# Linear attention and a gated MLP on one core: a lane layout of five and four tokens, the value products moved to VectorE, the first loads on two queues, and an earlier output weight load

## The chip, the cores and the metric

The kernel runs on one core of a Trainium2 chip. The metric is the device time of one execution, in microseconds (us). Six names recur: PE is TensorE (PEld its weight load), DVE is VectorE, ACT is ScalarE, POOL is GpSimd, SP is SyncE, which here only issues DMAs. A name with a q behind it (SPq, ACTq, POOLq) is that engine's instruction queue, where DMAs are issued. A lane is one of the 128 partitions of the on-chip memory.

## The reference

Attention with 8 batches, 8 heads, 576 tokens and a head size of 64, with cosine and sine weights over the token's position and no softmax; its result goes through an RMS norm and a gated MLP (512 to 1536 and back).

```python
def phi(x, c, s):                       # c, s = cos, sin of pi/2 * position / 576
    r = np.maximum(x, 0.0)
    return np.concatenate([r * c, r * s], axis=-1)
q_p, k_p = phi(q, cos_w, sin_w), phi(k, cos_w, sin_w)
kv = np.einsum('bhsf,bhsd->bhfd', k_p, v)
z = np.sum(k_p, axis=2)
num = np.einsum('bhsf,bhfd->bhsd', q_p, kv)
den = np.einsum('bhsf,bhf->bhs', q_p, z)[..., None] + 1e-06
x = (num / den).transpose(0, 2, 1, 3).reshape(8 * 576, 512)
xn = x / np.sqrt(np.mean(x * x, axis=-1, keepdims=True) + 1e-06) * rms_g
g = xn @ w_gate
return (g * (1.0 / (1.0 + np.exp(-g))) * (xn @ w_val)) @ w_out
```

## The kernel before

**Tokens and lanes.** A batch has 576 tokens. The first 512 lie four to a lane over 128 lanes (`J = 4`, token 4p + j in lane p) and arrive in one DMA for each of v, k and q (lines 72 to 78 and 97 to 108; q of the first two batches in two parts). The remaining 64 tokens of a batch come in DMAs of their own: v and k into tiles of 64 lanes (`vrem`, `krem`, line 80), q of two batches into one tile of 128 lanes (`qrem`, line 110). All these loads are issued by SP, in the order of the program, except `vrem` and `krem` of batch 0, which ACT issues (lines 119 and 120).

**A batch's attention.** `k_feat` (line 233) takes the relu of k, on ACT, for batches 0 and 1 in part on DVE. `v_trig` (line 243) multiplies v by the cosine (c = 0) and by the sine (c = 1) of the token's position: on DVE, but for batches above 0 the sine half is on POOL (line 245). There are ten such products a batch, two for each of the five token columns. `kv_mm` (line 251) is 40 matmuls a batch, `kv_evict` copies the result out. `q_relu` and a transpose (by PE in batches 0 and 1, by DMA after that, `q_turn`, line 282) prepare q; `num_mm` (line 316) makes a tile of 128 tokens; `sin_part` on ACT and `cos_part`, `divide` on DVE finish it; `sumsq` needs ACT and then POOL for the power -0.5 (line 383, tile `rs`); `norm` (line 386) is DVE. The normed tile `xn` is transposed into `xnT`, by PE (`x_turn_pe`, line 401, with a copy by ACT or DVE) or by a DMA that SP issues (`x_turn`, line 394).

**The MLP.** Nine blocks of 512 tokens: block b holds the four tiles of batch b, block 8 the remaining tokens of all batches, two batches to a tile. A block has 12 steps. A step (line 606) makes one piece of the gate and one of the value product (`gps`, `vps`, three PSUM buffers), a silu on ACT, a product on DVE (`hT`, line 631), and from block 2 on four output matmuls of the block before (`out_mm`, line 453). Blocks 0 to 3 work on halves of 256 tokens (`HALVES`, line 598): the first six steps of blocks 1 to 3 need tiles 0 and 1 of the block, the last six tiles 2 and 3.

**Order.** It is written out by hand. The attention of batch 0 comes first, with idle matmuls (`warm_up`) between. Block 0 follows. Then comes `lead` (line 641): the attention of batch 1 up to three tiles, mixed with the 48 output matmuls of block 0. Steps are numbered g = 12 x block + step, so block 1 is steps 12 to 23 and block 2 begins with step 24. `at(g, list, ...)` hangs work on a step; within a step the lists run in the order sp, act0, dve0, transposes by DMA that are due (`x_turn_late`), the step's matmuls and silu, act1, dve1, the `hT` product, the output matmuls, pe. What is issued on one engine runs in this order.

**Loads beside it.** POOL issues the weight loads: gate and value thirds 0 and 1 once the last value product of batch 0 is done (line 710), thirds 2 at line 745, the three thirds of w_out in step 1 (`more_loads`, line 525). Behind these SP waits for the second third of w_out (`sp_after`, line 528) and then issues v, k, their rests and q of batch 1, and v, k and their rests of batch 2. q of batch 2 is issued in step 12, v and k of batch 3 in steps 15 and 16, q in step 20, v and k of batch 4 in steps 21 and 22. v and k have two buffers, q has one.

Of the kernel before, what the change touches and what calls it, by code (L numbers as in the profile page):

```python
# [10 lines left out]
FP32 = mybir.dt.float32  # L11
# [6 lines left out]
def kernel(  # L18
# [51 lines left out]
    kraw, vraw, qraw, kremt, vremt, qremt = {}, {}, {}, {}, {}, {}  # L70

    def load_main(src, b, name, pool, eng=nc.sync):
        t = pool.tile([P, H, J * D], FP32, name=name, tag=name)
        K(eng.dma_start(
            out=t[:, :, :],
            in_=src[b, :, 0:SM, :].rearrange("h (p j) d -> p h (j d)", j=J),
        ))
        return t

    def load_rem(src, b, name, eng=nc.sync):  # L80
        t = raw2.tile([R, H, D], FP32, name=name, tag=name)
        K(eng.dma_start(
            out=t[:, :, :], in_=src[b, :, SM:S, :].rearrange("h s d -> s h d")
        ))
        return t

    def load_v(b):
        vraw[b] = load_main(v, b, "vraw", raw2)

    def load_k(b):  # L90
        kraw[b] = load_main(k, b, "kraw", raw2)

    def load_kv_rem(b):
        vremt[b] = load_rem(v, b, "vrem")
        kremt[b] = load_rem(k, b, "krem")

    def load_q(b, parts=1):

        t = raw.tile([P, H, J * D], FP32, name="qraw", tag="qraw")
        jn = J // parts  # L100
        for o in range(0, J, jn):
            K(nc.sync.dma_start(
                out=t[:, :, o * D : (o + jn) * D],
                in_=q[b, :, 0:SM, :].rearrange("h (p j) d -> p h j d", j=J)[
                    :, :, o : o + jn, :
                ].rearrange("p h j d -> p h (j d)"),
            ))
        qraw[b] = t

    def load_q_rem(m):  # L110
        t = raw.tile([P, H, D], FP32, name="qrem", tag="qrem")
        for o in range(2):
            K(nc.sync.dma_start(
                out=t[o * R : (o + 1) * R, :, :],
                in_=q[2 * m + o, :, SM:S, :].rearrange("h s d -> s h d"),
            ))
        qremt[m] = t

    vremt[0] = load_rem(v, 0, "vrem", nc.scalar)
    kremt[0] = load_rem(k, 0, "krem", nc.scalar)  # L120
    load_v(0)
    load_k(0)
    load_q(0, 2)


    iota_i = consts.tile([P, 1], mybir.dt.int32, name="iota_i")
    nc.gpsimd.iota(iota_i[:, :], pattern=[[0, 1]], base=0, channel_multiplier=1)
    iota_f = consts.tile([P, 1], FP32, name="iota_f")
    nc.vector.tensor_copy(out=iota_f[:, :], in_=iota_i[:, :])
    NC5 = J + 1  # L130
    th = consts.tile([P, 2, NC5], FP32, name="th")
    trig = consts.tile([P, 2, NC5], FP32, name="trig")
    ang = math.pi / 2.0 / float(S)
    for j in range(J):
        nc.vector.tensor_scalar(
            out=th[:, 1, j : j + 1], in0=iota_f[:, :], scalar1=float(J) * ang,
            scalar2=float(j) * ang, op0=ALU.mult, op1=ALU.add,
        )
    for o in range(2):
        nc.vector.tensor_scalar(  # L140
            out=th[o * R : (o + 1) * R, 1, J : J + 1], in0=iota_f[o * R : (o + 1) * R, :],
            scalar1=ang, scalar2=float(SM - o * R) * ang, op0=ALU.mult, op1=ALU.add,
        )
# [6 lines left out]
    def cosc(j, lo=0, hi=P):  # L150
        return trig[lo:hi, 0, j : j + 1]

    def sinc(j, lo=0, hi=P):
        return trig[lo:hi, 1, j : j + 1]
# [20 lines left out]
    def clear_pads(u):  # L175
        nc.gpsimd.memset(rk[u][J][R:P, :, :], 0.0)
        nc.gpsimd.memset(vx[u][J][R:P, :, :, :], 0.0)
        for j in range(NC5):
            n = P if j < J else R
            for c in range(2):  # L180
                nc.gpsimd.tensor_copy(
                    out=vx[u][j][0:n, :, c, D:E],
                    in_=trig[0:n, c, j : j + 1].unsqueeze(2).to_broadcast([n, H, 2]),
                )
# [43 lines left out]
    def kv_src(b, j):  # L228
        if j < J:
            return (kraw[b][:, :, j * D : (j + 1) * D], vraw[b][:, :, j * D : (j + 1) * D], P)  # L230
        return kremt[b][:, :, :], vremt[b][:, :, :], R

    def k_feat(b, j, dve=False):
        rkk, _, n = kv_src(b, j)
        dst = rk[b % 2][j][0:n, :, :]
        if dve:
            K(nc.vector.tensor_scalar(
                out=dst, in0=rkk, scalar1=0.0, scalar2=None, op0=ALU.max
            ))
        else:  # L240
            K(nc.scalar.activation(out=dst, in_=rkk, func=AF.Relu))  # L241

    def v_trig(b, j, c):
        _, rv, n = kv_src(b, j)
        eng = nc.gpsimd if b > 0 and c == 1 else nc.vector
        K(eng.tensor_scalar(  # L246
            out=vx[b % 2][j][0:n, :, c, 0:D], in0=rv,
            scalar1=(cosc, sinc)[c](j, 0, n), scalar2=None, op0=ALU.mult,
        ))
# [20 lines left out]

    def q_relu(b, t, dve=False):
        rq = rqp.tile([P, H, D], BF16, name="rq", tag="rq")
        src = qraw[b][:, :, t * D : (t + 1) * D] if t < J else qremt[b // 2][:, :, :]
        if dve:
            K(nc.vector.tensor_scalar(
                out=rq[:, :, :], in0=src, scalar1=0.0, scalar2=None, op0=ALU.max
            ))
        else:
            K(nc.scalar.activation(out=rq[:, :, :], in_=src, func=AF.Relu))
        rqs[b, t] = rq  # L280
# [47 lines left out]
    def sin_part(key, lo=0, hi=P):  # L328
        tmp = post2.tile([P, H, E], FP32, name="tmp", tag="tmp")
        K(nc.scalar.activation(  # L330
            out=tmp[lo:hi, :, :], in_=att[lo:hi, :, E:W], func=AF.Copy,
            scale=sinc(key[1], lo, hi),
        ))
        tmps[key] = tmp

    def cos_part(key, lo=0, hi=P):
        if key not in xa:
            xa[key] = post.tile([P, H, E], FP32, name="xa", tag="xa")
        K(nc.vector.scalar_tensor_tensor(  # L339
            out=xa[key][lo:hi, :, :], in0=att[lo:hi, :, 0:E],  # L340
            scalar=cosc(key[1], lo, hi), in1=tmps.pop(key)[lo:hi, :, :],
            op0=ALU.mult, op1=ALU.add,
        ))
# [99 lines left out]

    def out_store(blk, jt, osb):
        if blk < B:
            dst = out[blk * S : blk * S + SM, :].rearrange("(p j) m -> p j m", j=J)[:, jt, :]
            K(nc.sync.dma_start(out=dst, in_=osb[:, :]))
        else:
            for o in range(2):
                r0 = (2 * jt + o) * S + SM  # L450
                K(nc.sync.dma_start(out=out[r0 : r0 + R, :], in_=osb[o * R : (o + 1) * R, :]))
# [73 lines left out]
    def more_loads():  # L525
        for c in range(NG):
            load_wo(c)
        sp_after(wo[0:1, n4, 0:1])
        load_v(1)
        load_k(1)  # L530
        load_kv_rem(1)
        load_q(1, 2)
        load_v(2)
        load_k(2)
        load_kv_rem(2)

    at(1, "pe", more_loads)

# [15 lines left out]
    at(12, "sp", load_q, 2)  # L554
    for j, g in enumerate((13, 14, 15, 15, 16)):
        prep_at(g, 2, j)
    for t in range(J):
        at(15 + t, "act1", q_feat, 2, t)
    kv_at(17, 2)
    for t, g in enumerate((18, 19, 22, 24)):  # L560
        tile_at(g, (2, t), [(2, 0, P)], 2, t, t < 2)
    at(15, "sp", load_v, 3)
    at(16, "sp", load_k, 3)
    at(17, "sp", load_kv_rem, 3)
    at(20, "sp", load_q, 3)
    for j, g in enumerate((23, 24, 25, 26, 27)):
        prep_at(g, 3, j)
    for t in range(J):
        at(26 + t, "act1", q_feat, 3, t)
    kv_at(28, 3)  # L570
    for t, g in enumerate((29, 30, 32, 34)):
        tile_at(g, (3, t), [(3, 0, P)], 3, t)


    for b in range(4, B):
        g1, g2, g3 = NNT * (b - 1), NNT * (b - 2), NNT * (b - 3)
        for o, f in ((2, load_v), (4, load_k), (6, load_kv_rem)):
            at(20 + o // 2 if b == 4 else g3 + o + (4 if b == 5 else 0), "sp", f, b)
# [3 lines left out]
        for t in range(J):  # L582
            at(g2 + 9 + t, "act1", q_feat, b, t)
        kv_at(g2 + (11 if b == 4 else 10), b)
# [4 lines left out]
    for m, (gl, gf, gn) in enumerate(((33, 39, 44), (45, 51, 56), (56, 62, 68), (72, 82, 85))):  # L589
        at(gl, "sp", load_q_rem, m)  # L590
        at(gf, "act1", q_feat, 2 * m + 1, J)
        tile_at(gn, (2 * m + 1, J), [(2 * m, 0, R), (2 * m + 1, R, P)], B, m)
# [48 lines left out]
    def lead():  # L641
# [26 lines left out]
        q_relu(1, 3)  # L668
        outs(24, 30)
# [25 lines left out]
        divide((1, 2))  # L695

# [9 lines left out]
    warm_up(68)  # L706
# [58 lines left out]
    for c in range(2):  # L765
# [14 lines left out]
        for o, eng in enumerate((nc.sync, nc.scalar)):  # L780
            r0 = (2 * (J - 1) + o) * S + SM
            K(eng.dma_start(out=out[r0 : r0 + R, cs], in_=osb[o * R : (o + 1) * R, cs]))
# [28 lines left out]
```

## Time and profile before

| what | value |
|---|---|
| median of 3 runs | 348.25 us (347.69 to 348.96) |
| the profiled execution's own time | 349.69 us |
| its span, first to last instruction | 347.9 us |
| PE busy | 331.3 us |
| DVE, ACT, POOL busy | 201.9, 180.6, 92.2 us |
| DMA | 50.22 MB, mean 144 GB/s |
| granted TensorE clock | 0.995 |

Busy time is the time in which an engine had an instruction in work. Shares over the whole span say little here, since the kernel has an attention start, blocks in which attention and MLP share the engines, and late blocks that are almost only matmuls; so the views below are read by stretches of time, each counted from the start of the span. The granted clock is 1.00 in nearly all stretches, which means that nothing held TensorE back.

### The profile page before, as it was taken

What the parts mean: (1) busy time and instruction counts of PE and PEld (TensorE: products, weight loads), DVE (VectorE), ACT (ScalarE), POOL (GpSimd) and SP (SyncE); (2) the same over time, 40 slices, a digit from 0 to 9 for tenths busy, and PEclk for the clock granted to TensorE, in tenths of its full rate; (3) what the DMA queues carried; (4) which work ended last, traced back from release to release, by engine and by line L of the source; (5) the groups of instructions that cost most, each with busy time, mean ns of one, the idle gap of its engine ahead of it and who ended that gap; (6) DMA issues with size and microseconds to landing.
All of it is one profiled execution on the core that took longest, in us unless ns stands there. A gap on an engine that the chain in (4) does not pass through costs nothing.

```text
span 347.9 us, 6475 instructions
## 1 busy us (share of the span) xinstructions
PE 331.3 (95%) x2498; PEld 195.6 (56%) x2498; DVE 201.9 (58%) x362; ACT 180.6 (52%) x345; POOL 92.2 (27%) x116
## 2 busy tenths in 40 slices
PE   8779998979899999999999999999999999999995
PEld 6558854758677767777544444444444444444443
DVE  2885467765784887776668666864673352232210
ACT  1475337756566586655765576566544343323321
POOL 8433091560455264140514051400100000000000
PEclk9999999989999999999999999999999999999999
DMA  7999999778913998984399446224123011110024
GB/s 210 272 199 193 216 272 292 225 214 170 332 29 92 271 246 168 288 196 106 91 317 184 107 79 179 60 70 109 51 61 62 32 38 39 50 40 32 30 59 92
DMA packets 79424, 50.22 MB, mean 144 GB/s; under 512 B 43298, under 2 KB 74786, under 8 KB 79394
## 3 DMA queue, kind: packets, MB, share of 16 engines
q1 hardware_dynamic: 73426, 44.71, 51.7%
q0 software_dynamic: 4752, 4.72, 8.4%
q10 hardware_dynamic: 1216, 0.39, 0.6%
q8 instruction: 19, 0.31, 0.4%
q14 instruction: 11, 0.09, 0.1%
HBM read 38.01 MB, written 9.44 MB: 136 GB/s over the span
## 4 chain that ended last, share of the span: by engine, by line
PE 66%; POOL 8%; DMA 7%; issue 7%; DVE 6%; ACT 3%; SPq 1%; ACTq 0%; POOLq 0%; DVEq 0%
PE acc L461 20%; PE gps L423 16%; PE vps L423 15%; POOL vx L246 6%; PE gps L436 5%; PE vps L436 5%; DMA qraw<-in_q_dram 3%; PE att L320 3%; DMA wo<-in_moe_w_out_dram 3%; PE att L256 2%; POOL rs L383 2%; DMA vraw<-in_v_dram 2%; DVE xa L339 1%; ACT sq L378 1%; DVE xn L388 1%
## 5 line engine op out<-in xcount | busy, mean ns | idle before, releaser
L631 DVE TENSOR_TENSOR hT<-vps,sil 128x512 bf16<-128x512 f32 x108 | 74.4, 689 | 91.8 <-PE vps L423 62.0
L461 PE MATMUL acc<-wo,hT 128*128 128x512 bf16 x420 | 105.6, 379 | 0.0
L625 ACT ACTIVATE sil<-gps 128x512 bf16<-128x512 f32 x108 | 64.2, 595 | 79.0 <-PE gps L423 54.8
L383 POOL TENSOR_TENSOR rs<-ss,mhalf 128x1 f32<-128x1 f32 x36 | 20.3, 565 | 174.2 <-ACT sq L378 174.2
L461 PEld LDWEIGHTS <-hT 128*128 128x128 bf16 x420 | 40.7, 98 | 43.2
L436 PE MATMUL vps<-xnT,wv 128*128 128x256 bf16 x384 | 50.6, 276 | 1.1 <-DVE hT L631 1.1
L436 PE MATMUL gps<-xnT,wg 128*128 128x256 bf16 x384 | 50.7, 276 | 0.8 <-ACT xnT L414 0.7
L423 PE MATMUL gps<-xnT,wg 128*128 128x512 bf16 x192 | 49.5, 380 | 0.0
L423 PE MATMUL vps<-xnT,wv 128*128 128x512 bf16 x192 | 49.3, 379 | 0.0
L246 POOL TENSOR_SCALAR vx<-vraw,trig 128x512 bf16<-128x512 f32 x28 | 45.4, 1631 | 13.9 <-DMA vraw<-in_v_dram 13.9
L436 PEld LDWEIGHTS <-wg 128*128 128x128 bf16 x384 | 36.1, 99 | 9.5 <-issue 0.8
L436 PEld LDWEIGHTS <-wv 128*128 128x128 bf16 x384 | 37.9, 99 | 6.1 <-issue 1.5
L388 DVE SCALAR_TENSOR_TENSOR xn<-x,rs,gb 128x512 bf16<-128x512 f32 x36 | 32.7, 908 | 11.9 <-POOL rs L383 11.8
L423 PEld LDWEIGHTS <-wv 128*128 128x128 bf16 x240 | 23.5, 98 | 28.3
L339 DVE SCALAR_TENSOR_TENSOR xa<-att,trig,tmp 128x528 f32<-128x528 f32 (+1 forms) x40 | 30.5, 763 | 14.9 <-ACT tmp L330 13.9
L330 ACT ACTIVATE tmp<-att,trig 128x528 f32<-128x528 f32 (+1 forms) x40 | 28.0, 700 | 19.9 <-PE att L320 19.0
L423 PEld LDWEIGHTS <-wg 128*128 128x128 bf16 x240 | 21.8, 98 | 25.8
L467 ACT COPY osb<-acc 128x512 f32<-128x512 f32 x35 | 20.4, 583 | 25.8 <-PE acc L461 25.7
L378 ACT ACTIVATE sq<-x 128x513 f32<-128x513 f32 x36 | 22.6, 629 | 8.1 <-DVE x L365 7.8
L365 DVE TENSOR_TENSOR x<-xa,rec 128x512 f32<-128x512 f32 x36 | 24.9, 692 | 1.2
L246 DVE TENSOR_SCALAR vx<-vraw,trig 128x512 bf16<-128x512 f32 x36 | 20.5, 593 | 0.0
L241 ACT ACTIVATE rk<-kraw 128x512 bf16<-128x512 f32 x28 | 17.2, 624 | 3.4 <-DMA kraw<-in_k_dram 3.4
(54 smaller groups left out, 211.3 us busy)
## 6 DMA issues: line engine op xcount, KB each, us to landing
vraw<-in_v_dram SPq DMA_DIRECT2D x8, 1024.0 KB, 8.3
kraw<-in_k_dram SPq DMA_DIRECT2D x8, 1024.0 KB, 10.1
out_dram<-osb SPq DMA_DIRECT2D x32, 256.0 KB, 2.4
qraw<-in_q_dram SPq DMA_DIRECT2D x6, 1024.0 KB, 6.2
qraw<-in_q_dram SPq DMA_DIRECT2D x4, 512.0 KB, 10.6
wg<-in_moe_w_gate_dram POOLq DMA_DIRECT2D x3, 512.0 KB, 7.2
wv<-in_moe_w_val_dram POOLq DMA_DIRECT2D x3, 512.0 KB, 9.0
wo<-in_moe_w_out_dram POOLq DMA_DIRECT2D x3, 512.0 KB, 9.1
```

Source lines behind the costliest of these rows:

```text
L246: K(eng.tensor_scalar(out=vx[b % 2][j][0:n, :, c, 0:D], in0=rv, scalar1=(cosc, sinc)[c](j, 0, n), scalar2=None, op0=ALU.mult,))
L330: K(nc.scalar.activation(out=tmp[lo:hi, :, :], in_=att[lo:hi, :, E:W], func=AF.Copy, scale=sinc(key[1], lo, hi),))
L339: K(nc.vector.scalar_tensor_tensor(out=xa[key][lo:hi, :, :], in0=att[lo:hi, :, 0:E], scalar=cosc(key[1], lo, hi), in1=tmps.pop(key)[lo:hi, ...
L365: K(nc.vector.tensor_tensor(out=x[:, 0:DM].rearrange("p (s e d) -> p e s d", e=2, d=D), in0=a[:, :, 0:D].rearrange("p (e s) d -> p e s d", ...
L378: K(nc.scalar.activation(out=sq[:, :], in_=xs[key][:, :], func=AF.Square, scale=1.0 / math.sqrt(DM), accum_out=ss[:, :],))
L383: K(nc.gpsimd.tensor_tensor(out=rs[:, :], in0=ss[:, :], in1=mhalf[:, :], op=ALU.pow))
L388: K(nc.vector.scalar_tensor_tensor(out=xn[:, :], in0=xs.pop(key)[:, 0:DM], scalar=rss.pop(key)[:, :], in1=gb[:, :], op0=ALU.mult, op1=ALU. ...
L423: K(nc.tensor.matmul(ps[:, :], lhsT=w[:, dt, nn * P : (nn + 1) * P], rhs=xnT[blk][:, dt, :], start=(dt == 0), stop=(dt == NDT - 1),))
L436: K(nc.tensor.matmul(ps[:, i * HB : (i + 1) * HB], lhsT=w[:, dt, (n0 + i) * P : (n0 + i + 1) * P], rhs=xnT[blk][:, dt, hf * HB : (hf + 1) ...
L461: K(nc.tensor.matmul(acc[blk][:, :], lhsT=hT[blk][:, nn, jt * P : (jt + 1) * P], rhs=wo[:, nn, :], start=(nn == 0), stop=(nn == NNT - 1),))
L625: K(nc.scalar.activation(out=sil[:, :], in_=gp[:, :], func=AF.Silu))
L631: K(nc.vector.tensor_tensor(out=dst, in0=a, in1=c, op=ALU.mult))
```

## The change

The lanes hold tokens differently: 64 lanes hold five tokens each and 64 lanes four, so that the whole batch lies in one tile of five columns (the fifth is filled in 64 lanes only). Even batches have the five in lanes 0 to 63, odd ones in lanes 64 to 127. The loads of the remaining tokens go away. Each load is now two DMAs, one for 64 lanes, since the two halves have different strides; both are issued by SP, one behind the other, but for v and k of batch 0, where SP issues one half and ACT the other. Each store of an output tile of blocks 0 to 7 is two DMAs of 64 lanes as well. All value products are on DVE. The relu of the fifth column of q is done on DVE into tiles of its own. w_out's first third is issued at the end of step 0, and SP waits for that third, not for the second, before it issues the loads of batch 1. q of batch 2 is issued in `lead`; the eight value products and two relus of k of batch 2 stand at the end of `lead`, the rest of its preparation in steps 12 and 13. The matmuls of its `kv` move from step 17 to 14, its tiles from steps 18, 19, 22, 24 to 16, 18, 20, 22; the first two of them are transposed by DMA, as the others, and not by PE. q of batch 3 is issued in step 19, its tiles begin a step earlier. There are 60 idle matmuls at the start in place of 68.

```diff
-    def load_main(src, b, name, pool, eng=nc.sync):
...
+    FIVE = R * (J + 1)
+    FOUR = R * J
+    def halves(b):
+        if b % 2 == 0:
+            return ((0, 0, J + 1), (R, FIVE, J))
+        return ((0, 0, J), (R, FOUR, J + 1))
+    def load(src, b, name, pool, cuts=(0, J + 1), engs=(nc.sync, nc.sync)):
+        t = pool.tile([P, H, (J + 1) * D], FP32, name=name, tag=name)
+        for lo, hi in zip(cuts[:-1], cuts[1:]):
+            for (l0, t0, jn), eng in zip(halves(b), engs):
+                a, z = min(lo, jn), min(hi, jn)
+                K(eng.dma_start(
+                    out=t[l0 : l0 + R, :, a * D : z * D],
+                    in_=src[b, :, t0 : t0 + R * jn, :].rearrange(
+                        "h (p j) d -> p h (j d)", j=jn
+                    )[:, :, a * D : z * D],
+                ))
         return t
...
-    vremt[0] = load_rem(v, 0, "vrem", nc.scalar)
-    kremt[0] = load_rem(k, 0, "krem", nc.scalar)
-    load_v(0)
-    load_k(0)
-    load_q(0, 2)
+    two = (nc.sync, nc.scalar)
+    load_v(0, engs=two)
+    load_k(0, engs=two)
+    load_q(0, cuts=(0, 2, J + 1))
...
     def v_trig(b, j, c):
-        _, rv, n = kv_src(b, j)
-        eng = nc.gpsimd if b > 0 and c == 1 else nc.vector
-        K(eng.tensor_scalar(
+        _, rv, lanes = kv_src(b, j)
+        K(nc.vector.tensor_scalar(
...
     def out_store(blk, jt, osb):
...
+        for l0, dst in rows:
+            K(nc.sync.dma_start(out=dst, in_=osb[l0 : l0 + R, :]))
...
     def more_loads():
-        for c in range(NG):
+        for c in range(1, NG):
             load_wo(c)
-        sp_after(wo[0:1, n4, 0:1])
+        sp_after(wo[0:1, 0, 0:1])
         load_v(1)
         load_k(1)
-        load_kv_rem(1)
-        load_q(1, 2)
+        load_q(1)
         load_v(2)
         load_k(2)
-        load_kv_rem(2)
-
+    at(0, "pe", load_wo, 0)
     at(1, "pe", more_loads)
+    at(1, "dve1", q_relu, 0, J, True)
...
-    at(12, "sp", load_q, 2)
-    for j, g in enumerate((13, 14, 15, 15, 16)):
-        prep_at(g, 2, j)
+    for j in (2, 3):
+        at(12, "dve1", k_feat, 2, j, True)
+    at(12, "act1", k_feat, 2, J)
+    for c in range(2):
+        at(13, "dve0", v_trig, 2, J, c)
+    kv_at(14, 2)
     for t in range(J):
-        at(15 + t, "act1", q_feat, 2, t)
-    kv_at(17, 2)
-    for t, g in enumerate((18, 19, 22, 24)):
-        tile_at(g, (2, t), [(2, 0, P)], 2, t, t < 2)
+        at(14 + t, "act1", q_feat, 2, t)
+    at(17, "dve1", q_relu, 2, J, True)
+    for t, g in enumerate((16, 18, 20, 22)):
+        tile_at(g, (2, t), [(2, 0, P)], 2, t)
     at(15, "sp", load_v, 3)
     at(16, "sp", load_k, 3)
-    at(17, "sp", load_kv_rem, 3)
-    at(20, "sp", load_q, 3)
-    for j, g in enumerate((23, 24, 25, 26, 27)):
+    at(19, "sp", load_q, 3)
+    for j, g in enumerate((22, 23, 24, 25, 26)):
...
-        at(26 + t, "act1", q_feat, 3, t)
-    kv_at(28, 3)
-    for t, g in enumerate((29, 30, 32, 34)):
+        at(24 + t, "act1", q_feat, 3, t)
+    at(27, "dve1", q_relu, 3, J, True)
+    kv_at(27, 3)
+    for t, g in enumerate((28, 30, 32, 34)):
...
     def lead():
...
         q_relu(1, 3)
+        q_relu(1, J, dve=True)
+        load_q(2)
         outs(24, 30)
...
         divide((1, 2))
+        k_feat(2, 0)
+        k_feat(2, 1)
+        for j in range(J):
+            for c in range(2):
+                v_trig(2, j, c)
...
-    warm_up(68)
+    warm_up(60)
```

## The prediction

> **What bounds the kernel now.** I read the page's head first, then the busy time by stages, then chain, waits and SP's queue in the early stages.
>
> ```profile
> PE 331.3 (95%) x2498; PEld 195.6 (56%) x2498; DVE 201.9 (58%) x362; ACT 180.6 (52%) x345; POOL 92.2 (27%) x116
> ...
> 0.00:23.00 23.00, 18.21 (x189) 13.69 (x190) 14.46 (x40) 8.79 (x16) 13.30 (x44) 1.00 1.04 232
> 23.00:45.70 22.70, 21.84 (x204) 19.29 (x203) 11.49 (x19) 10.65 (x20) 5.50 (x7) 1.00 1.10 217
> 45.70:63.40 17.70, 15.47 (x139) 7.82 (x137) 12.88 (x25) 10.11 (x20) 8.39 (x7) 1.00 1.04 269
> 63.40:94.80 31.40, 27.36 (x281) 21.94 (x282) 21.15 (x37) 20.28 (x40) 13.67 (x11) 0.95 0.85 235
> 94.80:131.80 37.00, 36.32 (x362) 26.37 (x359) 28.33 (x50) 24.15 (x49) 17.35 (x14) 1.00 0.75 160
> 131.80:332.70 200.90, 200.90 (x1273) 100.47 (x1270) 112.52 (x192) 103.89 (x197) 34.00 (x35) 1.00 0.43 103
> ```
>
> The stages are the start, block 0, `lead`, block 1, block 2 and the rest; columns: length, busy time of PE, PEld, DVE, ACT, POOL, granted clock, DMA share, GB/s. From 131.8 on PE never idles and the matmuls stay the same, so nothing can be won or lost there. All is decided before. PE lacks 0.9 us in block 0, 2.2 in `lead`, 4.0 in block 1 (whose clock of 0.95 costs 31.4 x 0.05 = 1.6 more) and 0.7 in block 2, and the first gate matmul comes only after 23 us. What it waits for:
>
> ```profile
> 3.65 11.42 DMA qraw<-in_q_dram
> 28.86 9.07 DMA wo<-in_moe_w_out_dram
> 38.76 5.42 DMA vraw<-in_v_dram
> 44.28 8.71 POOL vx L246 x5
> ...
> PE att L256 <- POOL vx L246: 1.6, 2, 1.1
> DVE rq L275 <- DMA qraw<-in_q_dram: 1.6, 1, 1.6
> ```
>
> The first four are the chain of work that ended last: the start hangs on the second part of q (landed at 15.07), `lead` on w_out, v and five POOL products. The waits are those of `lead`: the change removes the first, the second stays. DMA is the other limit: its share is above 1.0 up to 63.4, so how fast the loads run matters as much as the order.
>
> **The price of a half.** Every load becomes two DMAs of 64 lanes, one behind the other. The nearest rows are output stores, where the last block already writes 64 lanes at a time (windows: a load of 128 lanes, v of batch 1; a store of 128 lanes; two pairs of 64-lane stores; last, two 64-lane loads in 256-byte packets):
>
> ```profile
> 41.00:46.00 5.00, 5.00 (x47) 4.39 (x45) 1.83 (x4) 1.79 (x3) 1.72 (x2) 1.00 1.06 357
> 335.00:335.80 0.80, 0.80 (x6) 0.33 (x4) 0.00 (x0) 0.00 (x0) 0.00 (x0) 1.00 0.87 328
> 338.00:339.40 1.40, 1.40 (x8) 0.60 (x7) 0.00 (x0) 0.58 (x1) 0.00 (x0) 1.00 0.85 187
> 340.50:341.90 1.40, 1.40 (x11) 0.97 (x10) 0.00 (x0) 0.50 (x1) 0.00 (x0) 1.00 0.86 187
> 188.10:189.10 1.00, 1.00 (x7) 0.43 (x5) 1.00 (x3) 1.00 (x3) 1.00 (x2) 1.00 1.31 252
> ```
>
> The same 0.26 MB take 0.8 us as one store and 1.4 us as two halves. A load of v, k or q is now 576 x 512 x 4 bytes = 1.18 MB: 3.3 us at 357 GB/s, 4.7 at 252, 6.3 at 187. I take 5.6 us (210 GB/s, the mean of six 0.2 us windows inside the first pair: 225, 215, 184, 185, 236, 215), since that pair has the new loads' form; 3.3 and 6.3 are kept as ends. [...]
>
> **The start.** v and k of batch 0 come over two queues. Nearest is the stretch from 5 to 10 us, where ACT's queue loads 64 lanes beside SP's 128: 200 to 303 GB/s, mean 270. From the first packets at 2.8 us, 2.36 MB take 8.7 us at that rate: 11.5, against 11.75 (1.25 + 10.5) before. So v and k cost nothing, and 8 fewer idle matmuls nothing either; ends: 357 GB/s gains 2.1 us, 187 loses 3.9. Eleven small position instructions in place of eight end before 4 us, under the wait for v (DVE idle until 7.65). Then q on SP alone: 0.52 MB 2.5 us, 0.66 MB 3.1 us, so the second part lands at 11.3 + 5.6 + 0.4 = 17.3, which is 2.2 us late. DVE's relu of it stands ahead of two `rqT` copies and the first `cos_part`; what it lacks, all lack. The first weight loads run from 14.4 on, beside it. Between 14.4 and 15.2 the DMA view has
>
> ```profile
> q0 software_dynamic: 71, 0.07, 63.8%
> q1 hardware_dynamic: 76, 0.12, 44.6%
> ```
>
> packets of weights (q0) and SP's queue (q1) one for one; if that held, the part would land up to 6 us later still. I take **+2.2** and keep -1.7 (all at 357) and +8.
>
> **w_out in step 0** gains nothing by itself: POOL's `rs` at 27.35 (0.78 us) stands before it in either step, so it is issued at 28.1 as now. But SP waits for third 0, landed 6.9 us after issue, at 35.0, not for third 1 at 37.95. First packets of v then come at 37.6, 3 us earlier.
>
> **`lead`.** With 5.6 us a load the queue's data end: v 43.2, k 48.8, q 54.4, v of batch 2 60.0, k 65.6. The products of batch 1 on DVE take 8 x 0.41 (3.24 us for eight in the start) from 46.66: all ten are done by 51.7 with two relus between. POOL's chain ended at 53.0, so `kv` could be done 1.4 us sooner. It is of no use: q lands at 54.8, against 52.4, and `num_mm` follows it. `lead` ends 2.4 us later, at 65.8. The q relu of the fifth column (0.45 us) fits where DVE waits 1.6 us for `tmp`. If q came early the 1.4 us would be won.
>
> **Block 1.** ACT first waits for k of batch 2 (66.0), then two relus: silu of step 12 at 67.2. DVE, after `divide` at 66.8, has eight products (3.3), two relus (0.8), `hT` (0.6), `norm` (0.7): 72.2. Queued behind is the PE transpose of tile (1,2), which also needs the PSUM buffer that this `hT` frees: PE goes on at 72.6, some 2.6 us after it could. Afterwards DVE has fewer products than now, POOL's 3.3 us pairs are gone, and so is the 1.18 us `xn` beside them (0.74 alone). With matmuls of 0.87 us, step 24 would be due at 93.0.
>
> But two tiles of batch 2 are now transposed by DMA, in SP's queue. What it costs to stand behind a load there:
>
> ```profile
> 74.36 0.57 SPq L74 DMA_DIRECT2D kraw<-in_k_dram  x1
> 75.42 1.19 SPq L284 DMA_TRANSPOSE rqT<-rq  x1
> ```
>
> The first `rqT`, ahead of any load, landed after 2.5 us, this one after 5.5, with the k load (5.8 us). In the new order SP issues v3 (v of batch 3, step 15, 75.6), `rqT`, k3, two `rqT`, q3 (step 19), `xnT` of tile (2,0), v4 (step 21), `xnT` of tile (2,1). First packets 1.8 us after issue: 77.4, four loads 22.4, five transposes at 0.76 us (512 packets each, as in lone ones) 3.8: the last lands at **103.6**. Step 24 needs tiles (2,0) and (2,1). It began at 94.8: **+8.8 us**. Now the cover is that both go through PE, for 0.8 us.
>
> **The rest.** Block 2 loses its 0.7 us of PE idle (POOL pairs, `xn`): **-0.7**, or 0. Later blocks have 18 us of loads and 5.6 of stores in 31 us, and a tile is due 7.8 us after its last turn: hidden. The 32 added store DMAs (0.36 us of SP each) are covered by that slack too, and 22 issues of rests go. Eight relus of the fifth q column move to DVE (0.45 us each) and four leave ACT, in steps that last 2.6 us and in which both idle. The tail's stores stay as they are.
>
> Sum: 2.2 + 8.8 - 0.7 = +10.3 us on the profiled execution's 349.69 us (span 347.9 and 1.8 around it). That execution is 1.4 above the median of the runs; on the median, 348.25 + 10.3 = **358.5 us**.
>
> **Rivals.** (a) Halves run as fast as whole loads. Then the start gains 1.0 (within -1.7), `lead` 1.4, block 1 3.6 (PE's own 24.7 us + 2.6 + 0.5 against 31.4), block 2 0.7, and `xnT` is about 1 us late: -5.7, **342.5**. It decides where a load takes under some 4.1 us (287 GB/s; a straight line between the two sums). For it: 252 GB/s in the only load row above. Against it: 187 in the rows of the same form. (b) 4.7 us a load, as that row has: q costs nothing, the last transpose lands at 72.5 + 1.8 + 18.8 + 3.8 = 96.9, +2.1, the start +1, block 2 -0.7: **350.6**. (c) Two queues help v and k no more than one: at 187 GB/s k lands 3.9 us later and v 1.9, and with v's products the weight loads start 1.9 later, which q then meets less: +3 net, **361.5**. [...] (d) Loads are fast, but DVE becomes the bound of block 1: its 21.15 us lose 4.8 (products there, slow `xn`) and gain 10.2 (ten products 4.7, relus 1.3, a tile 2.3, batch 3's four 1.9), 26.6 against PE's 24.7, and weights meet q at the start: about **347.5**.
>
> **Chances.** Forecast 0.40, (a) 0.27, (b) 0.11, (c) 0.13, (d) 0.09. A measurement of this kernel can tell about 0.3% from no change. Faster: (a) and a third of (d), 0.30; within 0.3%: 0.06; slower 0.64. Range 341.5 to 364.0; the forecast's own 352 to 364.
>
> **What would show it.** GB/s near 200 while v of batch 1 loads, 5 us and more from one landing to the next; q's second part at 17 us; ACT waiting for `kraw` at the end of `lead`; and PE idle for 8 us before step 24 with `xnT` as releaser. Loads at 350 GB/s, or `xnT` landed before PE comes to step 24, would make the prediction wrong.

## The result and the profile after

The changed kernel takes **384.0 us** (median of 4 runs, 382.1 to 385.7) where the kernel before takes 348.61: a ratio of **1.102**, 95% interval 1.095 to 1.108. It is slower, and by 35 us where 10 were forecast. The profiled execution took 382.1 us, its span 380.3 against 347.9. The busy line of its page:

```profile
PE 334.4 (88%) x2449; PEld 198.3 (52%) x2482; DVE 209.6 (55%) x410; ACT 177.3 (47%) x337; POOL 34.2 (9%) x82
```

Its busy time by stages, cut at the same work as those of before (start, block 0, `lead`, blocks 1 and 2, rest; the same columns):

```profile
0.00:28.30 28.30, 19.76 (x182) 14.82 (x183) 16.27 (x44) 9.31 (x18) 12.85 (x45) 0.82 1.07 208
28.30:50.07 21.77, 21.58 (x201) 19.16 (x201) 10.90 (x18) 10.02 (x19) 3.56 (x5) 1.00 1.15 191
50.07:74.89 24.82, 16.70 (x135) 8.32 (x136) 13.69 (x31) 9.95 (x20) 1.10 (x2) 0.86 1.13 219
74.89:117.97 43.08, 27.33 (x280) 21.61 (x281) 28.25 (x59) 20.66 (x41) 2.92 (x5) 0.88 0.94 164
117.97:162.61 44.64, 37.12 (x346) 27.09 (x353) 24.99 (x50) 23.72 (x45) 2.19 (x4) 0.92 0.85 147
162.61:365.00 202.39, 200.78 (x1246) 101.28 (x1270) 114.38 (x207) 100.94 (x191) 11.60 (x21) 0.99 0.54 99
```

PE's work is nearly the same (334.4 us busy against 331.3), so most of the loss is waiting. The first cut above lies on the first gate matmul (28.30); the one of before lies 0.94 us ahead of it (23.00, the matmul at 23.94). Counted from that matmul in both, the start is 4.4 us longer, block 0 equal, `lead` 7.1 longer, block 1 11.7, block 2 7.6, and the rest with the last microseconds behind the table 1.6: together 32.4, the difference of the spans. Two columns belong together: the DMA share is as high as before or higher, yet the bytes of the start, block 0 and `lead` move at 191 to 219 GB/s and not at 217 to 269. The engines are as busy and move less. And the granted clock, 1.00 in nearly every stage of before, is 0.82 to 0.92 in four stages. What ended the waits stands in the chain, here the longest piece of four of its stretches (start and length in us),

```profile
8.61 10.15 DMA qraw<-in_q_dram
44.96 17.35 DMA qraw<-in_q_dram
104.99 12.85 DMA xnT<-xn
152.26 10.31 DMA xnT<-xn
```

and in the waits (total, times, longest):

```profile
PE gps L441 <- DMA xnT<-xn: 16.2, 2, 9.1
ACT rk L243 <- DMA kraw<-in_k_dram: 21.7, 3, 9.7
```

The waits of POOL's products that stood in `lead` are gone. In their place stand loads (q of batch 0 landing at 18.8 us, q of batch 1 at 62.3) and two transposes by DMA that PE waits for, 9.1 us before step 24 and 7.1 us before step 36.

### The profile page after: what moved, and what is told of

Its sections match the earlier page's. It is cut to its first block, busy times and chain, and to the rows that moved or that the text cites. A ratio compares the mean times of both kernels' runs of the same rounds, so it can differ in the third digit from the quotient of the medians.

```text
span 380.3 us, 6453 instructions
## 1 busy us (share of the span) xinstructions
PE 334.4 (88%) x2449; PEld 198.3 (52%) x2482; DVE 209.6 (55%) x410; ACT 177.3 (47%) x337; POOL 34.2 (9%) x82
## 4 chain that ended last, share of the span: by engine, by line
PE 70%; DMA 16%; DVE 6%; ACT 2%; SPq 2%; issue 2%; POOL 0%; ACTq 0%; DVEq 0%
PE acc L473 21%; PE gps L428 14%; PE vps L428 13%; PE gps L441 9%; PE vps L441 8%; DMA qraw<-in_q_dram 7%; DMA xnT<-xn 6%; PE att L325 3%; DMA rqT<-rq 2%; SPq L89 2%; PE att L257 1%; DVE vx L247 1%; DVE hT L646 1%; DVE xn L393 1%; DVE xa L344 1%
## 5 line engine op out<-in xcount | busy, mean ns | idle before, releaser
L640 ACT ACTIVATE sil<-gps 128x512 bf16<-128x512 f32 x108 | 64.3, 596 | 95.3 <-PE gps L428 55.4
L473 PE MATMUL acc<-wo,hT 128*128 128x512 bf16 x401 | 103.4, 381 | 1.0 <-issue 0.2
L441 PE MATMUL gps<-xnT,wg 128*128 128x256 bf16 x384 | 52.5, 282 | 17.0 <-DMA xnT<-xn 16.2
L441 PE MATMUL vps<-xnT,wv 128*128 128x256 bf16 x384 | 52.2, 281 | 0.0
L441 PEld LDWEIGHTS <-wg 128*128 128x128 bf16 x384 | 36.8, 101 | 26.9 <-issue 10.2
L441 PEld LDWEIGHTS <-wv 128*128 128x128 bf16 x384 | 38.8, 101 | 5.6
L428 PEld LDWEIGHTS <-wv 128*128 128x128 bf16 x240 | 23.5, 98 | 28.3
L247 DVE TENSOR_SCALAR vx<-vraw,trig 128x512 bf16<-128x512 f32 (+1 forms) x80 | 34.2, 478 | 6.1 <-DMA vraw<-in_v_dram 5.9
L479 ACT COPY osb<-acc 128x512 f32<-128x512 f32 x35 | 20.4, 584 | 30.0 <-PE acc L473 28.1
L393 DVE SCALAR_TENSOR_TENSOR xn<-x,rs,gb 128x512 bf16<-128x512 f32 x36 | 27.0, 749 | 9.1 <-POOL rs L388 8.5
L243 ACT ACTIVATE rk<-kraw 128x512 bf16<-128x512 f32 (+1 forms) x34 | 20.8, 623 | 21.8 <-DMA kraw<-in_k_dram 21.7
L370 DVE TENSOR_TENSOR x<-xa,rec 128x512 f32<-128x512 f32 x36 | 24.9, 692 | 1.2
L325 PE MATMUL att<-kvm,rqT 64*128 64x132 bf16 x320 | 16.9, 226 | 5.7 <-DMA rqT<-rq 3.7
```

Source lines behind the costliest of these rows:

```text
L247: K(nc.vector.tensor_scalar(out=vx[b % 2][j][lanes, :, c, 0:D], in0=rv, scalar1=(cosc, sinc)[c](b, j, lanes), scalar2=None, op0=ALU.mult,))
L325: K(nc.tensor.matmul(att[:, e * NP + pr, 0:W], lhsT=rqT[key][e * D : (e + 1) * D, pr, :], rhs=kvm[b % NK][e * D : (e + 1) * D, pr, :], sta ...
L370: K(nc.vector.tensor_tensor(out=x[:, 0:DM].rearrange("p (s e d) -> p e s d", e=2, d=D), in0=a[:, :, 0:D].rearrange("p (e s) d -> p e s d", ...
L393: K(nc.vector.scalar_tensor_tensor(out=xn[:, :], in0=xs.pop(key)[:, 0:DM], scalar=rss.pop(key)[:, :], in1=gb[:, :], op0=ALU.mult, op1=ALU. ...
L428: K(nc.tensor.matmul(ps[:, :], lhsT=w[:, dt, nn * P : (nn + 1) * P], rhs=xnT[blk][:, dt, :], start=(dt == 0), stop=(dt == NDT - 1),))
L441: K(nc.tensor.matmul(ps[:, i * HB : (i + 1) * HB], lhsT=w[:, dt, (n0 + i) * P : (n0 + i + 1) * P], rhs=xnT[blk][:, dt, hf * HB : (hf + 1) ...
```

## The experiments

The start of the first silu of each block, from ACT's timeline, is the ruler for all of them (us):

| kernel | block 0 | block 1 | block 2 | block 3 | block 4 |
|---|---|---|---|---|---|
| before | 25.0 | 65.1 | 95.8 | 133.0 | 168.4 |
| the change | 29.4 | 77.0 | 119.9 | 164.6 | 200.7 |
| b_lane_halves | 31.7 | 79.9 | 113.3 | 155.5 | 192.7 |
| a_whole | 24.9 | 66.9 | 101.7 | 141.5 | 178.5 |
| a_whole_pe | 25.1 | 67.1 | 96.2 | 134.4 | 169.9 |
| a_mend | 25.4 | 65.7 | 96.4 | 132.7 | 168.2 |
| a_pe_turn | 30.1 | 79.1 | 112.7 | 157.2 | 193.5 |
| a_two | 28.0 | 77.3 | 121.2 | 159.4 | 194.8 |
| b_dve | 24.6 | 65.7 | 93.3 | 129.7 | 165.2 |
| b_dve_wo | 25.5 | 64.3 | 92.0 | 128.6 | 164.1 |

### How a load is cut

Three kernels are the kernel before with one edit: every load of 512 tokens is two DMAs on SP, cut in another way each.

```diff
-        K(eng.dma_start(out=t[:, :, :], in_=SRC))
+        for ln, hs in PIECES:
+            K(eng.dma_start(out=t[ln, hs, :], in_=SRC[ln, hs, :]))
# b_lane_halves: lanes 0-63, then 64-127     b_evenodd: even lanes, then odd lanes
# b_head_halves: 128 lanes, heads 0-3, then heads 4-7
```

**b_lane_halves**

> The kernel before, with one edit: each load of v, k and q (the 512 tokens) is two DMAs on SP, lanes 0 to 63 and lanes 64 to 127. T1 (a DMA to 64 neighbouring lanes runs at about 205 GB/s, as the changed kernel's loads did): a 1.05 MB load takes 5.1 us in place of 2.9; the start loses about 5 us, lead and block 1 about 10 together, so 365 us (355 to 375). T2 (any load cut in two is slow, by number or size of DMAs): the same. T3 (the loss is in the rest of the change, the order of block 1 and the products on VectorE): at most 355 us.

**b_head_halves**

> The kernel before, with each load of v, k and q as two DMAs on SP of 128 lanes and four heads each: as many DMAs, packets and bytes as in the lane halves. T1: within 2 us of the kernel before, 346 to 351, and 340 GB/s or more while v of batch 1 loads. T2: as slow as the lane halves, 355 us or more.

**b_evenodd**

> The kernel before, with each load of v, k and q as two DMAs on SP of 64 lanes, the even ones and the odd ones. T1 (it is the neighbourhood of the lanes): near the kernel before, 346 to 353, over 300 GB/s while v of batch 1 loads. T1b (it is the number of 64 lanes): as the lane halves, 355 to 375 at about 205 GB/s.

Measured: b_lane_halves 370.87 us, ratio 1.057 (1.050 to 1.065); b_head_halves 349.22, 0.996 (0.993 to 1.000); b_evenodd 352.82, 1.005 (1.000 to 1.010). A stretch in which only loads run, in each of the three in that order:

```profile
50.00:56.00 6.00, 6.00 (x43) 3.93 (x41) 2.87 (x6) 1.19 (x2) 1.22 (x1) 1.00 1.12 200
```

```profile
41.00:46.00 5.00, 5.00 (x47) 4.39 (x45) 1.90 (x3) 1.79 (x3) 0.22 (x1) 1.00 1.07 359
```

```profile
41.00:46.00 5.00, 5.00 (x47) 4.40 (x46) 1.93 (x3) 1.79 (x3) 0.00 (x0) 1.00 1.01 331
```

Two DMAs in place of one cost nothing (359 GB/s by heads, 357 in one DMA), and 64 lanes in a DMA cost nothing much either, as long as they are every other lane: 331 GB/s. The same 64 lanes as neighbours load at 200. The DMA share is above 1.0 in all three (1.12, 1.07 and 1.01): the engines are occupied, only with slower packets. From these shares and rates (share x 16 engines / rate), a 1 KB packet holds an engine for an estimated 92 ns in lane halves, 49 by heads and 50 in even and odd lanes. So it is which lanes, not how many.

### The change with whole loads

**a_whole** keeps all of the change's order and its products on VectorE, but loads and stores as before: 512 tokens in one DMA of 128 lanes, and the rest of a batch in a small second DMA into the fifth column.

```diff
-        for (l0, t0, jn), eng in zip(halves(b), engs):   # two DMAs of 64 lanes
+        K(engs[0].dma_start(out=t[:, :, 0 : J * D], in_=SRC))            # 128 lanes
+        K(engs[1].dma_start(out=t[fives(b), :, J * D :], in_=REST))      # 64 tokens
```

> The changed kernel with all of its order, but v, k and q are loaded as before: 512 tokens four to a lane in one DMA of 128 lanes, the 64 others by a small DMA into the fifth column of their 64 lanes; output stores of 128 lanes again. T1: the stalls go, 340 to 349 us, first matmul of block 2 before 95 us. T3 (order and VectorE products cost by themselves): 360 us or more.

Measured 359.98 us, 1.024 (1.017 to 1.031). The start is what it was (24.9), but a loss of some 9 us stays, and T1's 340 to 349 us are missed: the loads alone are not the cause. With 9 us from this kernel and 20 from b_lane_halves, most of the 35 us is accounted for. That the 6 us left over come from both meeting is an inference; no run separates them. PE's timeline shows where the 9 us are:

```profile
99.75 1.87 PE L449 MATMUL gps<-xnT,wg 128*128 128x256 bf16 x8 [4.98 <-DMA xnT<-xn]
140.35 1.05 PE L449 MATMUL gps<-xnT,wg 128*128 128x256 bf16 x8 [2.58 <-DMA xnT<-xn]
```

Step 24 waits 5 us for a transpose behind loads even with fast loads, and the eight matmuls behind it take 1.87 us where 1.04 is usual.

**a_whole_pe** sends the first two tiles of batch 2 through TensorE again, as before the change:

```diff
-        tile_at(g, (2, t), [(2, 0, P)], 2, t)
+        tile_at(g, (2, t), [(2, 0, P)], 2, t, t < 2)
```

> The changed order with the loads whole again, as in the run before, and besides that the first two tiles of batch 2 turned by TensorE and not by DMA. Theory A (what is left of the loss hangs on the DMA turns that stand behind loads): the 4.98 us wait at 99.75 us goes, PE's turns add 0.8, and some 1 us of halved clock behind the wait goes too: 354 to 356 us against 359.98. Rival B (it hangs on VectorE's queue at the end of lead, ten products and two relus ahead of step 12): the wait at step 24 only changes its name, from xnT to xn or xps, and the time stays at 358.5 to 360.5. Either way the 2.58 us wait before step 36 should still be there, since that tile is still turned by DMA.

Measured 351.71 us, 1.005 (1.000 to 1.010): 8.3 us less than a_whole (some 7 by the two ratios), more than expected. The wait before step 24 is gone, no stretch at half clock is left (mean granted clock 1.00 against 0.984), and the wait before step 36, still 2.37 us, no longer has such a stretch behind it either. VectorE's queue (rival B) does not take over: its 2.02 us wait for `xn` is there in both kernels, in place of the 1.63 of before.

**a_mend** has besides q of batch 1 in two parts, and the first two tiles of batch 3 through TensorE.

```diff
-        load_q(1)
+        load_q(1, cuts=(0, 2, J))
-        tile_at(g, (3, t), [(3, 0, P)], 3, t)
+        tile_at(g, (3, t), [(3, 0, P)], 3, t, t < 2)
```

> The changed order with whole loads and batch 2's first two tiles turned by TensorE (351.71), and besides q of batch 1 in two parts as before (its wait was 2.42 us) and batch 3's first two tiles turned by TensorE too (wait 2.37, turns 0.8). Theory A (these two waits are what is left between it and the kernel before): 351.7 - 2.4 - 1.6 = 347.7 us. Rival B (VectorE's queue at the end of lead, the 2.02 us wait for xn, takes over what q frees): 349 to 351.

Measured 348.7 us, 0.995 (0.991 to 0.999), between the two expectations: those two waits go, the one for `xn` stays at 1.9. Against the kernel before, the whole costs nothing any more and gains little. But it holds the products on VectorE and the earlier w_out, and with these two alone b_dve_wo (below) takes 345.34 us: its slowest run, 346.84, is faster than the fastest of a_mend, 347.08. So the new lane layout and order still cost some 3 us. By the table block 0 and `lead` together are 1.5 us longer and block 1 is 3.0: PE waits 2.3 us there for `rqT`, and runs at half clock for 3.4 us around the matmuls behind it.

### The change as it is, with one thing mended

**a_pe_turn** is the changed kernel with the same two tiles of batch 2 through TensorE (the edit of a_whole_pe).

> The changed kernel as it is, in halves of neighbouring lanes, with only the first two tiles of batch 2 turned by TensorE. Theory A: the wait of 9.12 us before step 24 goes and with it about 1.9 us of matmuls at half clock behind it; the two turns cost 0.8: 384 - 9.1 - 1.9 + 0.8 = 374 us. Rival C (in blocks 1 to 3 the loads are the bound, and PE only meets the backlog at another place): block 3 begins earlier but its xnT lands no earlier, so the 7.1 us wait before step 36 grows by what step 24 saved: 379 to 384 us. A result between 375 and 379 says that both are in it, and the wait before step 36 tells how much.

Measured 375.39 us, 1.071 (1.062 to 1.080). The wait before step 24 is gone; the one before step 36 is

```profile
155.25 1.86 PE L441 MATMUL gps<-xnT,wg 128*128 128x256 bf16 x8 [6.50 <-DMA xnT<-xn]
```

6.5 us where it was 7.1. It did not grow by what step 24 saved, so theory A holds (1.4 us above its 374; the table has 2.1 us more ahead of block 1, where the two kernels do the same work): the two waits are two places with the same order (a transpose issued behind loads), not one backlog that moves.

**a_warm** puts idle matmuls into both waits of the changed kernel.

```diff
+        if g in IDLE:                       # IDLE = {24: 76, 36: 56}
+            idle_mm(IDLE[g])
```

> The changed kernel with idle matmuls added in PE's two longest waits: 76 before step 24 (8.1 us of the 9.1 us wait) and 56 before step 36 (6.0 of 7.1). Nothing else differs. Theory G (PE's granted clock is halved because PE stands idle, and what it costs is the work behind the wait): the clock stays at 1.00 through both, block 2 becomes 1.9 us shorter and block 3 1.5 us, 380 to 381 us against 384.0. Rival H (the halved clock comes from elsewhere, or the loads go on to decide): no gain, 383 to 385. The landings of both xnT tiles should stay where they are, at 118.0 and 162.6 us, in the second case 1.9 earlier.

Measured 382.02 us, 1.091 (1.083 to 1.099), which overlaps the interval of the change itself: the gain in time is not resolved. In the trace the two places came out differently:

```profile
120.09 1.04 PE L441 MATMUL gps<-xnT,wg 128*128 128x256 bf16 x8
164.27 1.05 PE L441 MATMUL gps<-xnT,wg 128*128 128x256 bf16 x8 [2.03 <-DMA xnT<-xn]
165.15 1.69 PE L441 MATMUL vps<-xnT,wv 128*128 128x256 bf16 x8
```

Behind step 24's wait the clock stayed at 1.00 and the group took 1.04 us, not 1.87: the half clock does come from PE's standing idle. At step 36 the idle matmuls ended 2.03 us too soon, and the clock was halved again for 3.4 us. Yet block 2 became only 0.5 us shorter and not 1.9. From step 24's start to that of the last matmuls ahead of step 36 it took 34.6 us and not 36.2, but then the tile for step 36 was awaited, and PE went on 44.2 us after step 24's start where it had been 44.6. What the half clock cost ahead of this wait was largely hidden in it.

### The parts that were thought harmless

**b_dve** and **b_wo** are the kernel before with one edit each, **b_dve_wo** has both.

```diff
# b_dve
-        eng = nc.gpsimd if b > 0 and c == 1 else nc.vector
+        eng = nc.vector
# b_wo
-        for c in range(NG):
+        for c in range(1, NG):
             load_wo(c)
-        sp_after(wo[0:1, n4, 0:1])
+        sp_after(wo[0:1, 0, 0:1])
+    at(0, "pe", load_wo, 0)
```

> The kernel before with one edit: all value products on VectorE, none on GpSimd. Theory A (this part of the change is sound, and takes 1.6 us of waits for POOL out of lead and 0.7 out of block 2): VectorE's xn in blocks 1 and 2 falls from some 0.9 us to 0.75, POOL falls from 92 to about 35 us busy, and the time is 346.5 to 349.5 against some 349 for the kernel before. Rival D (VectorE becomes the bound in blocks 1 and 2, where five more products a batch of 0.48 us come on 20 us of busy time): PE waits for hT or xn more than before, 351 to 355 us.

> The kernel before with one edit: the first third of w_out issued at the end of step 0, and SP's loads of batch 1 released by that third, not by the second. Theory A (nothing is won by it): v of batch 1 starts 3 us earlier but shares the 16 DMA engines with thirds 1 and 2 of w_out, so k and q land at most 1 us earlier and w_out's last third up to 2 us later: 348 to 350 us, within 0.3% of the kernel before. Rival E (the first packets decide): q of batch 1 lands 2 to 3 us earlier, lead's waits go: 346 to 347.5. Rival F (w_out late): lead begins later, 350.5 to 352.

> The kernel before with the two edits of the change that won by themselves: all value products on VectorE (ratio 0.9885) and w_out's first third in step 0 with SP released by it (0.9959). If both gains add up: about 0.9844, 344 to 345 us where before is 349.5 to 350. Rival (they win the same wait at the end of lead): no better than 346.3, that of the products alone.

Measured: b_dve 346.27 us, **0.989** (0.983 to 0.994); b_wo 348.35, 0.996 (0.992 to 1.000); b_dve_wo 345.34, **0.987** (0.981 to 0.993). The products on VectorE are a gain; the earlier w_out is one of at most 0.8%; that both add up is not resolved. In b_dve VectorE has hardly more to do than before (201.9 us), since much of what is added is given back by its other instructions, which POOL's products no longer slow: a norm took 908 ns, a product 593, and now 750 and 478:

```profile
PE 330.6 (96%) x2498; PEld 194.8 (57%) x2498; DVE 203.2 (59%) x397; ACT 180.2 (52%) x345; POOL 35.2 (10%) x81
...
L388 DVE SCALAR_TENSOR_TENSOR xn<-x,rs,gb 128x512 bf16<-128x512 f32 x36 | 27.0, 750 | 8.5 <-POOL rs L383 7.7
L246 DVE TENSOR_SCALAR vx<-vraw,trig 128x512 bf16<-128x512 f32 x64 | 27.4, 478 | 0.0
```

In the chain of b_dve_wo eight products of batch 1 follow one another:

```profile
47.50 3.16 DVE vx L246 x8
```

The chain of before has five products on POOL in that place, 8.71 us.

### Halves by themselves, and on two queues

**b_ladder** measures single loads after the kernel's last store.

```diff
+    def rung(*parts):
+        t = raw.tile([P, H, J * D], FP32, name="rung", tag="qraw")
+        for eng, ln, hs in parts:
+            K(eng.dma_start(out=t[ln, hs, :], in_=SRC[ln, hs, :]))
```

> The kernel before, and after its last store a ladder of loads into one buffer, each of which waits until the one before has landed (the tiles are read by nothing; the results are those of before). Each rung is 1.05 MB (512 tokens of q, 1 KB packets) or a half or quarter of it. [...]

From a rung's first DMA packet to its last, in us: whole 3.9 and 3.8; lane halves on SP 5.5; lane halves on SP and ACT 5.5; even and odd lanes 3.7, on two queues 3.8; half the heads on each of two queues 3.7. Half the bytes: lanes 0 to 63 2.9, lanes 64 to 127 3.1, even lanes 2.1, lanes 32 to 95 2.3. A quarter: lanes 0 to 31 1.4, every fourth lane 1.5. So 64 neighbours that reach over both halves (32 to 95, 2.3 us) come nearer to the even lanes (2.1) than to lanes 0 to 63 (2.9): neighbourhood alone does not make a load slow. But every fourth lane (1.5) is no faster than lanes 0 to 31 (1.4): for a quarter, spreading over the lanes gains nothing. What property of the lanes sets the rate, these times do not show. The two queues were no test: ACT's half moved its first packets when SP's was nearly done.

**b_ladder2** has up to four loads under way at a time.

```diff
+    def rung(cut, parts):
+        for n in range(4):
+            t = raw2.tile([P, H, J * D], FP32, name="rung", tag=("vraw", "kraw")[n % 2])
+            for h in range(0, H, cut):
+                for eng, ln in parts:
+                    K(eng.dma_start(out=t[ln, h : h + cut, :], in_=SRC[ln, h : h + cut, :]))
```

> The kernel before, and after its last store seven groups of four loads of 1.05 MB, up to four under way at a time (nothing reads them; the results are those of before). Groups 1, 2 and 7 whole, in one DMA; group 3 in neighbouring halves on SP's queue; group 4 lower halves on SP's and upper halves on ACT's queue; group 5 as 3 but cut finer, two heads of one half and two of the other by turns; group 6 lower halves on SP's and upper halves on POOL's queue. [...] Rival T2c (halves serialize whichever queues they are on): groups 3 to 6 all at 190 to 210.

Whole loads, halves on one queue, then three stretches with halves on SP's and on ACT's queue, and the finer cut on one queue:

```profile
358.00:370.00 12.00, 0.00 (x0) 0.00 (x0) 0.00 (x0) 0.00 (x0) 0.00 (x0) 0.50 1.09 348
374.00:384.00 10.00, 0.00 (x0) 0.00 (x0) 0.00 (x0) 0.00 (x0) 0.00 (x0) 0.50 1.14 202
387.00:390.00 3.00, 0.00 (x0) 0.00 (x0) 0.00 (x0) 0.00 (x0) 0.00 (x0) 0.50 1.14 191
392.00:394.00 2.00, 0.00 (x0) 0.00 (x0) 0.00 (x0) 0.00 (x0) 0.00 (x0) 0.50 1.10 334
400.00:403.00 3.00, 0.00 (x0) 0.00 (x0) 0.00 (x0) 0.00 (x0) 0.00 (x0) 0.50 1.09 336
409.00:414.50 5.50, 0.00 (x0) 0.00 (x0) 0.00 (x0) 0.00 (x0) 0.00 (x0) 0.50 1.12 234
```

In the third to fifth row both queues carry a good share each (SP and ACT 0.28 and 0.29 MB, 0.33 and 0.34, 0.55 and 0.46), and the sum is 191 in the first and 334 and 336 in the others. Counting SP's bytes shows why. From 348.7 to 373.2 us its queue moved the 8.39 MB of the eight whole loads, and there the rate falls from 350 to 200 GB/s. Then come the eight halves of group 3, 0.52 MB each, lower and upper by turns, and the lower halves of group 4, while ACT's queue holds upper halves only and runs beside the end of group 3. SP had moved 2.79 MB of halves by 387 us and 3.07 by 390: it was in the sixth, an upper one, as ACT was. By 392 and 394 it had moved 3.32 and 3.65: the seventh, a lower one. By 400 and 403 it had moved 4.65 and 5.19: the first two of group 4, both lower. So two upper halves under way together ran at 191 GB/s, a lower and an upper one at 334 and 336. Rival T2c, 190 to 210 GB/s for all of groups 3 to 6, does not hold: 334 and 336 lie far above it, and group 5's 234, on one queue, lies above it too. (The count takes it that a queue moves its loads in the order of issue.) Group 6 was no test: POOL's halves fell beside the end of group 5, and SP's then ran alone, at 197 GB/s from 434 to 443 us.

**a_two** and **a_two_mend** put the upper halves of the changed kernel on a second queue, POOL's (ACT's for q of batch 0); a_two_mend has the mends of a_mend as well.

```diff
-    def load(src, b, name, pool, cuts=(0, J + 1), engs=(nc.sync, nc.sync)):
+    def load(src, b, name, pool, cuts=(0, J + 1), engs=(nc.sync, nc.gpsimd)):
-    load_q(0, cuts=(0, 2, J + 1))
+    load_q(0, cuts=(0, 2, J + 1), engs=two)
```

> The changed kernel with one edit: the upper half of every load from batch 1 on, and of q of batch 0, goes over a second queue (POOL's from batch 1 on, ACT's for q of batch 0), so that both halves can be under way together. Theory T1: loads run at 300 GB/s and more where both queues are busy, the start loses under 1 us against before, and the order costs what it did with whole loads (360): 357 to 364 us. Rival T2c (they serialize): 380 to 386 us. Rival J: POOL's power for rs waits behind its DMA issues (0.77 us each, and what they wait for), norm comes late: between the two, with PE waiting for xn.

> As a_two, and besides with the mends that took the changed order to 348.7 us with whole loads: the first two tiles of batches 2 and 3 turned by TensorE, q of batch 1 in two parts. By T1 347 to 354 us; by T2c (one queue's speed, without the waits at steps 24 and 36) 370 to 375; by J 352 to 362.

Measured 376.21 us, 1.073 (1.064 to 1.082), and 368.22, 1.052 (1.044 to 1.059): both between the theories' figures. From 42 to 53 us of a_two, when w_out was nearly through, the DMA view has 2.23 MB in 529 packets on POOL's queue and 0.53 MB in 525 packets on SP's, 252 GB/s in all. The two queues went packet for packet, and POOL's packets are four times as large (4.2 KB on average against 1.0). So its halves took most of the engines, SP's halves came last and then ran alone, at 204 GB/s from 56 to 64 us. Opposite halves were under way, but the two queues did not share evenly, and `lead` did not become shorter. POOL's `rs` (rival J) was no visible cause: `norm` waited 9.1 us for it in all, 8.5 in the change.

## Where the prediction was right and where it failed

**Right: the direction, the price of a half, and the first mechanism.** Halves loaded at 200 to 208 GB/s (210 taken), k and q of batch 1 came 5.7 us apart (5.6 taken), ACT waited for `kraw`, and PE waited for `xnT` before step 24, 9.1 us where "8 us" was to be seen. w_out was issued at 28.1 counted with block 0's delay taken off, as said. Rivals (a), (b) and (d) all needed faster loads. VectorE as the bound of block 1 (d) did not come with whole loads either: in a_mend PE's longest wait for `xn` is 1.9 us beside 1.63 before. Rival (c) described the first 8 us of the start.

The sum was 10.3 us and came out at 32.4. Term by term:

- **The start, +2.2 taken, +4.4 measured.** "2.36 MB take 8.7 us" at 270 GB/s did not hold. ACT's half of v came first and alone, then SP's half alone; from 5.5 to 8 us the trace has 198 GB/s, and only from 9 to 11.5, with both queues under way, 340. k landed at 13.4 and not at 11.5, q's second part at 18.8 and not at 17.3. The matmuls behind it ran at half clock, since PE had waited 4.2 us for k, which adds an estimated 0.6.
- **`lead`, +2.4 taken, +7.1 measured.** The step that failed is "First packets of v then come at 37.6, 3 us earlier". SP did issue v early, at 39.55 (start's delay included), but the engines still had two thirds of w_out. The queues from 40 to 42 us (weights), then from 42 to 44 (weights, SP's loads):

```profile
q0 software_dynamic: 384, 0.38, 120.8%
...
q0 software_dynamic: 308, 0.30, 91.1%
q1 hardware_dynamic: 185, 0.19, 28.9%
```

  v was done at 50.9 and not at 45.4 (43.2 and the start's 2.2). An earlier issue into a full machine is no earlier load; k and q only followed. a_whole, with whole loads, lost 1.9 us here, so most of the 7.1 are the halves'.
- **Block 1, +6.4 taken (8.8 less lead's 2.4), +11.7 measured.** The mechanism was right: a tile that goes by DMA behind four loads. v of batch 3 was issued 2.1 us later after the start of block 1 than reckoned, and from that issue to the landing it took 31.0 us, not 28.0.
- **Block 2, -0.7 taken, +7.6 measured**, the worst step: "Later blocks have 18 us of loads and 5.6 of stores in 31 us, and a tile is due 7.8 us after its last turn: hidden." That weighed a sum of loads against a block's length. But SP had put q of batch 4 and v and k of batch 5 ahead of the transpose, which was issued at 152.26 and landed 10.3 us later. With whole loads the same place waits 2.4 to 2.6. The slack of a block says nothing of the place in the queue.
- **The clock was not in the sum at all**, though the prediction had priced the 0.95 of block 1 before (one stretch of 3.4 us at half clock) at 1.6 us. After the waits PE ran at half clock: 3.4 us behind step 24, 3.1 behind step 36, 3.3 in `lead` and 3.4 behind the `rqT` wait of block 1. Half of that is work not done, 1.7 + 1.5 + 1.6 + 1.7, with the start's 0.6 some 7 us beside the 22 that were missing. That is an upper bound for the time it cost: in a_warm the clock kept behind step 24 shortened block 2 by 0.5 us. Where no later wait hides it, it counts: in a_whole_pe a wait of 5.0 us taken away brought 7 to 8.

The range's upper end (364.0) came from the terms that were bounded, each by itself. Block 2, which had been called hidden, had no bound, and the largest miss was there.

## What to carry to other kernels

Look at which lanes a DMA touches before its size: a cut into two runs of 64 neighbouring lanes cost over 40% of the rate (200 GB/s against 357), a cut into even and odd lanes or by heads almost nothing. If it must be two runs of neighbours, they belong on two queues with packets of about one size, so that a lower and an upper run are under way together (334 and 336 GB/s in b_ladder2, 340 in the start of the change; 252 in a_two, where one queue had packets of 4.2 KB and the other of 1.0). A transfer that PE needs must not be issued behind bulk loads on the same queue, whatever the block's slack in bytes (the transpose for step 36 of the change took 10.3 us to land, the median of the transposes before was 3.2); where it could be done by TensorE for under 1 us (0.4 us of matmuls a tile here), it should. And price a wait of PE at up to 1.7 us more than its length: that much was lost at half clock behind each of the long ones, unless a later wait hides it.

## What was not expected of the hardware

- Neighbouring or alternate lanes: 200 GB/s (b_lane_halves) against 331 (b_evenodd) for the same 64 lanes a DMA and the same 1 KB packets. For half the bytes as one load, b_ladder has 2.9 and 3.1 us for lanes 0 to 63 and 64 to 127, 2.1 for the even lanes and 2.3 for lanes 32 to 95; for a quarter, every fourth lane (1.5 us) is no faster than lanes 0 to 31 (1.4).
- Two halves on two queues moved 191 GB/s while both were upper halves, and 334 and 336 while one was a lower and one an upper half (b_ladder2). Whole loads had 348 there, and halves by turns on one queue 202.
- The granted clock fell to 0.50 around waits of PE of 2.03 us (a_warm), 2.29 (a_mend), 2.58 (a_whole), 3.7 and more (the change), but not around one of 2.59 (a_whole, in `lead`) and one of 2.37 (a_whole_pe). So the length of the wait alone did not decide it. The stretches at half clock, though, have few lengths: 10.2, 6.8, 3.4, 10.2 and 6.8 us in the change, 6.8 and 3.4 in a_whole, 3.4 in a_mend and in the kernel before, all whole multiples of 3.4. What sets these lengths, no run shows.
